# Attention pieces of four heads: the value product turned round onto two column tiles of the array

## The chip, the cores and the metric

The kernel runs on one core of a Trainium2 chip. The metric is the device time of one execution in microseconds (us). A core has a matrix engine (PE, with its weight loads listed apart as PEld), a vector engine (DVE), a scalar engine (ACT), a general engine (POOL, also called GpSimd) and a queue that issues transfers (SP). They run side by side and wait for each other through semaphores. On PE a product takes a stationary operand, loaded first, and a moving operand, streamed through it; the result lands in PSUM, from which DVE and ACT read. All other tiles lie in SBUF.

## The reference

Eight heads of causal attention over 8 batches of 576 positions (head dimension 64), four heads with a local window of 32, four with a strided mask, and then a two-layer network on the result.

```python
scores = scale * np.matmul(q, k.transpose(0, 1, 3, 2))
mask_local = (rel >= 0) & (rel < stride)
mask_strided = (rel >= 0) & (pos[None, :] % stride == pos[:, None] % stride)
...
scores = scores - np.max(scores, axis=-1, keepdims=True)
attn = np.exp(scores)
attn = attn / (np.sum(attn, axis=-1, keepdims=True) + 1e-09)
return np.matmul(attn, v).astype(np.float32)
...
h = x @ w_in                    # 4608 x 512 by 512 x 2048
sp = np.maximum(h, 0.0) + np.log1p(np.exp(-np.abs(h)))
g = h * erf(sp)
return (g @ w_out).astype(np.float32)
```

## The kernel before, in words

The network is cut into 12 chunks of 384 tokens, and each chunk into 16 slices of 128 hidden units: 192 steps, made by `ftile`. A step's `mm1` is 12 matrix products into a PSUM tile `h`. Eleven operations on ACT and DVE then work on the tiles `a` and `b` (DVE's are `n2`, `n5`, `n6`, `prod` and `split_lo`), and the result is split into a high part `ghi` (ACT) and a low part `glo` (DVE). A step's `mm2` is three times three products with `ghi` and `glo` stationary, into the three PSUM tiles `o`. There are three buffers of `h`: a fourth `mm1` can start only when `prod` (the last to read `h`, L682) has released the first.

Attention makes the network's input, `xhi` and `xlo`. Its masks leave only blocks near a diagonal (the strided heads after a reordering of positions), so a piece holds the scores of a few blocks of 96, 126 or 72 queries against 128 keys. Batches 0 and 1 go through `piece`, which is not altered beyond the names and sizes of buffers. Batches 2 to 7 go through `quad`: 36 pieces of four heads (two pairs), 18 with 96 queries to a block and 12 with 126 (two blocks to a pair, so eight head blocks, scores in two PSUM banks), and 6 with 72 queries (one block to a pair, four head blocks, one bank). Scores are stored with the keys on the partitions and the queries along the row, and a piece goes like this:

- `scores` (PE): in the two-bank pieces eight products, the two heads of a pair on the two 64-row tiles of the array.
- `mask` (DVE) adds the mask, `maxi` (POOL, a reduction over all partitions) takes the maximum over the keys, `sub` (DVE) subtracts it, `exp` (ACT).
- `av` (PE): the exponentials `sm` are stationary, the values `v` move. `v` has a 65th column of ones, so each product's last column is the sum of the exponentials. Queries come out on the partitions.
- `total`, `invert`, `scale` (DVE, for each pair): the sum plus 1e-9, its reciprocal, and the product of the two into `xn`.
- `transp` (PE): turns `xn` round, head dimensions onto the partitions, as `mm1` needs them.
- `split_hi` (ACT) and `split_lo_x` (DVE) write `xhi` and `xlo` from PSUM.

The order of all work is set by a planner in the kernel (`Plan`): every operation has a cost, a key and the operations it comes after, buffers are handed out by tag, and the planner lists each engine's instructions in the order of the starts that it works out. On the chip each engine then runs its list strictly in that order. Operations named in `TWO` (two SBUF operands on DVE) and POOL's are kept apart in the planned order (`locks`).

Of the kernel before, what the change touches and what calls it, by code (L numbers as in the profile page):

```python
# [18 lines left out]
P = 128  # L19
# [44 lines left out]
class Buf:  # L64
# [6 lines left out]
    def __getitem__(self, key):  # L71
        return self.tile[key]

# [95 lines left out]
def attention_moe(  # L169
# [31 lines left out]
    bufs = {"qk": 2, "v": 3, "sm": 3, "mx": 2, "xn": 2, "ps": 2, "h": 3, "a": 2, "b": 2, "ghi": 3, "glo": 3,  # L201
# [15 lines left out]
    def dve(n, x=1.0):  # L217
        return 0.067 + n * x / 960.0

    def act(n, fixed=0.093):  # L220
        return fixed + n / 1200.0


    def piece(b, hp, j, key, dt, ring, pe_mask=False, pool_sub=False, early=False):
# [168 lines left out]
    def quad(b, loc, j, key, dt, ring):  # L393
# [14 lines left out]
        sm = [buf("apool", "sm", [P, 4 * QS], f"sm{i}_{pid}") for i in range(nbank)]  # L408
        mx = [buf("apool", "mx", [P, 4 * QS], f"mx{i}_{pid}") for i in range(nbank)]
        pav = [buf("ps_a", "ps", [P, 512], f"av{i}_{pid}") for i in range(2)]  # L410
        xn = [buf("apool", "xn", [P, 4, D], f"xn{i}_{pid}") for i in range(2)]
        rc = [buf("apool", "r", [P, 4, 1], f"r{i}_{pid}") for i in range(2)]
        pt = buf("ps_a", "ps", [P, 512], f"t_{pid}")
# [79 lines left out]

        def av():
            for i in range(2):
                for u in range(units):
                    bank, c = place(i, u // 2, u % 2)
                    yield nc.tensor.matmul(  # L498
                        pav[i][:n, u * (D + 1) : (u + 1) * (D + 1)],
                        sm[bank][:, c : c + n],  # L500
                        v[i][:, u // 2, u % 2, :],
                        start=True,
                        stop=True,
                    )

        def norm(i):
            a, rr = lambda: pav[i][:n, : units * (D + 1)].rearrange("p (u d) -> p u d", u=units), lambda: rc[i][:n, :units]

            def total():
                yield nc.vector.tensor_scalar(  # L510
                    out=rr(), in0=a()[:, :, D : D + 1], scalar1=1e-9, scalar2=None, op0=ALU.add
                )

            def invert():
                yield nc.vector.reciprocal(rr(), rr())

            def scale():
                yield nc.vector.tensor_tensor(
                    out=xn[i][:n, :units], in0=a()[:, :, :D], in1=rr().broadcast_to([n, units, D]), op=ALU.mult
                )  # L520

            return total, invert, scale

        def transp():
            for i in range(2):
                for blk in range(nblk):
                    c = i * w + blk * n
                    yield nc.tensor.transpose(  # L528
                        pt[:, c : c + n], xn[i][:n, 2 * blk : 2 * blk + 2, :].rearrange("p h d -> p (h d)"), ident[:n, :n]
                    )  # L530

        def views(i, t):
            base, src = (b % 2) * S, pt[:, i * w : (i + 1) * w]
# [30 lines left out]
        o_v = add("pe", 0.00174 * n * 2 * units + 0.05, key + dt + 0.2, av, [*o_e, *lv], [*pav, *xn], [*sm, *v])  # L564
        o_n = []
        for i in range(2):
            total, invert, scale = norm(i)
            o = add("dve", 0.07, key + 1.5 * dt, total, [o_v], [rc[i]], [pav[i]])
            o = add("dve", 0.1, key + 1.5 * dt, invert, [o], [], [rc[i]])
            o_n.append(add("dve", dve(units * D), key + 1.5 * dt + 0.1, scale, [o], [], [pav[i], rc[i], xn[i]]))  # L570
        o_t = add("pe", 0.09 + 0.11 * 2 * nblk, key + 2 * dt, transp, o_n + ring, [pt], [*xn])
        done = []
        for i in range(2):
            hi, lo = split(i)
            o = add("act", act(w, 0.06), key + 2 * dt + 0.1, hi, [o_t], [], [pt])
            done.append(add("dve", dve(w), key + 2 * dt + 0.2, lo, [o], [], [pt]))
# [359 lines left out]
```

## Time and profile before

| | |
|---|---|
| median of 3 runs | 984.49 us (984.04 to 984.52) |
| profiled execution | 983.67 us, of which the span of its instructions is 981.9 us |
| PE busy | 970.0 us, 99% of the span |
| DVE busy | 720.9 us, 73% |
| ACT busy | 654.0 us, 67% |
| POOL busy | 146.4 us, 15% |
| granted PE clock | 1.00 throughout |

A row of the profile names line, engine, operation, output and inputs, shape, count, busy time and mean duration, and behind the last bar how long its engine stood idle before it and what ended that. Since records of one engine overlap (the next starts before the last one's end is written), a duration is a little longer than the time that an instruction adds; the distance from start to start in the timeline is what it adds. A product of plain 32-bit floats (`scores`, `av`) is recorded as two matmuls, a product of the network (on split parts) or a transpose as one.

### The profile page before, as it was taken

Reading aid. Unit: us, or ns where it says so; the run is one execution under the profiler, and the core shown is the slowest. Engines: PE = TensorE matmul, PEld = TensorE weight load, DVE = VectorE, ACT = ScalarE, POOL = GpSimd, SP = SyncE. Lnnn points to the kernel's source line nnn. Section 1 sums busy time; section 2 is a strip of 40 time slices with the busy share of each in tenths; the row PEclk is TensorE's granted clock in tenths of the full one; section 3 lists DMA queues with packets and bytes.
Section 4 is the critical chain, followed back from the end, with each engine's and each line's share of the span. In section 5 each row is a group of like instructions: output and inputs, shape, how many; then the busy total and the mean of one; then the engine's idle time right before and its main releaser. Section 6 shows DMA issues by size and latency. Waiting matters only on the chain.

```text
span 981.9 us, 15767 instructions
## 1 busy us (share of the span) xinstructions
PE 970.0 (99%) x5683; PEld 871.8 (89%) x5683; DVE 720.9 (73%) x1607; ACT 654.0 (67%) x1475; POOL 146.4 (15%) x94
## 2 busy tenths in 40 slices
PE   8999999999999999999999999999999999999998
PEld 6688989998899999899998989999999899999997
DVE  6999997776767777577778686667767776666664
ACT  4676777666757666666767666766756666766765
POOL 3534111111111311021011210111111210000000
PEclk9999999999999999999999999999999999999999
DMA  9994211012112221020221220211121210000000
GB/s 323 287 346 154 76 42 46 26 52 64 59 37 87 72 56 49 28 68 20 77 62 50 89 71 12 76 34 44 53 69 48 79 45 1 33 1 1 33 1 33
DMA packets 37661, 68.80 MB, mean 70 GB/s; under 512 B 4176, under 2 KB 18640, under 8 KB 37584
## 3 DMA queue, kind: packets, MB, share of 16 engines
q1 hardware_dynamic: 37584, 67.80, 21.6%
q8 instruction: 45, 0.74, 0.3%
q14 instruction: 32, 0.26, 0.1%
HBM read 58.34 MB, written 9.44 MB: 69 GB/s over the span
## 4 chain that ended last, share of the span: by engine, by line
PE 92%; DVE 6%; DMA 1%; issue 0%; ACT 0%; SPq 0%
PE h L647 40%; PE o L717 40%; PE av L498 5%; PE s L452 4%; DVE w L605 1%; DVE w L611 1%; PE t L528 1%; DVE pair L619 1%; DVE w L598 1%; PE s L265 1%; DMA words<-w_in 1%; PE av L308 1%; DVE xlo L362 0%; DVE a L652 0%; DMA qk<-qk_loc 0%; DVE b L652 0%
## 5 line engine op out<-in xcount | busy, mean ns | idle before, releaser
L717 PE MATMUL o<-pair,ghi 128*128 128x512 f32 x1152 | 364.2, 397 | 0.0
L647 PE MATMUL h<-xhi,pair 128*128 128x384 f32 x1536 | 305.5, 340 | 0.6 <-DVE b L682 0.6
L647 PEld LDWEIGHTS h<-xhi,pair 128*128 128x128 f32 x1536 | 271.2, 188 | 14.4 <-DVE b L682 1.6
L655 ACT ACTIVATE b<-b 128x384 f32<-128x384 f32 x384 | 198.9, 520 | 70.0 <-DVE b L652 67.8
L717 PEld LDWEIGHTS o<-pair,ghi 128*128 128x128 f32 x1152 | 208.5, 188 | 32.6
L717 PE MATMUL o<-pair,glo 128*128 128x512 f32 x576 | 225.2, 391 | 0.0
L476 POOL PARTITION_ALL_REDUCE mx<-sm x66 | 101.2, 1572 | 599.4 <-DVE sm L468 599.4
L647 PE MATMUL h<-xlo,pair 128*128 128x384 f32 x768 | 166.1, 337 | 0.0
L688 DVE TENSOR_TENSOR glo<-b,ghi 128x384 fp32r<-128x384 f32 x192 | 110.5, 576 | 60.7 <-ACT ghi L685 51.2
L685 ACT CAST ghi<-b 128x384 fp32r<-128x384 f32 x192 | 98.1, 511 | 79.3 <-PE o L717 73.1
L652 DVE SCALAR_TENSOR_TENSOR a<-h,a 128x384 f32<-128x384 f32 x192 | 106.2, 553 | 56.3 <-ACT a L655 55.4
L682 DVE TENSOR_TENSOR b<-b,h 128x384 f32<-128x384 f32 x192 | 105.1, 548 | 44.3 <-ACT b L655 43.9
L647 PEld LDWEIGHTS h<-xlo,pair 128*128 128x128 f32 x768 | 137.4, 187 | 0.0
L652 DVE SCALAR_TENSOR_TENSOR a<-a,h 128x384 f32<-128x384 f32 x192 | 105.5, 550 | 42.1 <-ACT b L655 40.3
L717 PEld LDWEIGHTS o<-pair,glo 128*128 128x128 f32 x576 | 108.1, 188 | 23.3
L655 ACT ACTIVATE b<-a 128x384 f32<-128x384 f32 x192 | 100.2, 522 | 40.2 <-DVE glo L688 39.2
L655 ACT ACTIVATE a<-h 128x384 f32<-128x384 f32 x192 | 92.9, 484 | 46.2 <-PE h L647 44.4
L655 ACT ACTIVATE a<-a 128x384 f32<-128x384 f32 x192 | 100.3, 522 | 35.1 <-DVE a L652 33.7
L652 DVE SCALAR_TENSOR_TENSOR b<-b,a 128x384 f32<-128x384 f32 x192 | 108.8, 567 | 3.1
L498 PEld LDWEIGHTS av<-v,sm 128*96 128x96 f32 (+2 forms) x528 | 54.2, 172 | 2.2
L291 POOL PARTITION_ALL_REDUCE mx<-sm x24 | 45.1, 1890 | 64.2 <-ACT sm L283 58.6
L498 PE MATMUL av<-v,sm 128*96 128x65 f32 (+2 forms) x528 | 53.3, 253 | 0.0
(48 smaller groups left out, 651.2 us busy)
## 6 DMA issues: line engine op xcount, KB each, us to landing
qk<-qk_loc SPq DMA_DIRECT2D x48, 304.0 KB, 3.1
qk<-qk_str SPq DMA_DIRECT2D x32, 380.0 KB, 3.7
v<-v_all SPq DMA_DIRECT2D x80, 130.0 KB, 2.2
out<-ob SPq DMA_DIRECT2D x36, 256.0 KB, 2.0
words<-w_in SPq DMA_DIRECT2D x16, 512.0 KB, 5.9
words<-w_out SPq DMA_DIRECT2D x16, 512.0 KB, 6.1
qk<-qk_str SPq DMA_DIRECT2D x16, 136.0 KB, 2.1
v<-v_all SPq DMA_DIRECT2D x16, 65.0 KB, 1.9
```

The costliest lines, as they stand in the source:

```text
L265: yield nc.tensor.matmul(dst, qk[:, k0 + blk * step : k0 + blk * step + P], qk[:, blk * 2 * n : (blk + 1) * 2 * n], start=blk == 0, stop=n ...
L291: yield nc.gpsimd.partition_all_reduce(mx[:, :cols], sm[:, :cols], P, ReduceOp.max)
L452: yield nc.tensor.matmul(s[bank][:, c : c + width], qk[i][rows, keys], qk[i][rows, q0 : q0 + width], start=bank not in used, stop=True, sk ...
L476: yield nc.gpsimd.partition_all_reduce(mx[k][:, :cols], sm[k][:, :cols], P, ReduceOp.max)
L498: yield nc.tensor.matmul(pav[i][:n, u * (D + 1) : (u + 1) * (D + 1)], sm[bank][:, c : c + n], v[i][:, u // 2, u % 2, :], start=True, stop= ...
L647: yield nc.tensor.matmul(ph[:, :CH], win[4 * s + cc][:, w, fs], x[cc][:, c0 : c0 + CH], start=(i == 0), stop=(i == len(terms) - 1))
L652: yield nc.vector.scalar_tensor_tensor(out=out, in0=in0, scalar=scalar, in1=in1, op0=op0, op1=op1)
L655: yield nc.scalar.activation(dst, src, func, bias=bias[i], scale=scale)
L682: yield nc.vector.tensor_tensor(out=bb.tile, in0=bb.tile, in1=ph[:, :CH], op=ALU.mult)
L685: yield nc.scalar.copy(ghi.tile, bb.tile)
L688: yield nc.vector.tensor_tensor(out=glo.tile, in0=bb.tile, in1=ghi.tile.bitcast(F32), op=ALU.subtract)
L717: yield nc.tensor.matmul(po.tile, g[:, ts], wout[f][:, w], start=(f == 0 and i == 0), stop=(f == NFC - 1 and i == 2),)
```

## The change: what it does

In `quad` the value product is turned round. `v` (128 keys by 64 columns, without the ones) is stationary and the exponentials move; the two heads of a pair write to partitions 0 to 63 and 64 to 127 of one PSUM tile `px`, so they use the two 64-column tiles of the array in turn. The result has head dimensions on the partitions already, and `transp` goes. The sums come from POOL: a second reduction over all partitions, `add` in place of `max`, on the exponentials of each bank, into `su`. Every partition then holds the same row of sums. DVE turns the sums by 32x32 transposes (`gather`, 64 partitions at a time), adds 1e-9 and takes the reciprocal of one column per block (`invert`), and spreads the result over the rows with one more transpose (`spread`). One DVE product (`scale`) writes the normalised piece from PSUM into the SBUF tile `tt`, and `split_hi` and `split_lo_x` read `tt` instead of PSUM. That an earlier chunk has been read out of `xhi` and `xlo` (`ring`) is now waited for by `split_hi` on ACT, where it was by `transp` on PE. `ghi` and `glo` go from three buffers to two; `tt` and `inv` share two.

```diff
-    bufs = {... "xn": 2, "ps": 2, "h": 3, "a": 2, "b": 2, "ghi": 3, "glo": 3,
+    bufs = {... "tt": 2, "ps": 2, "h": 3, "a": 2, "b": 2, "ghi": 2, "glo": 2,
...
+        def total(k):
+                yield nc.gpsimd.partition_all_reduce(su[k][:, :cols], sm[k][:, :cols], P, ReduceOp.add)
+        def gather(h):
+                if pos > n:
+                    yield nc.vector.memset(t[rows, cols : cols + pos - n], 1.0)
...
+                for u in range(2 * nblk):
+                    yield nc.vector.transpose(
+                        tt[rows, u * pos : (u + 1) * pos], t[rows, lo + u * step : lo + u * step + pos]
+                    )
+        def invert():
+            yield nc.vector.tensor_scalar(
+                out=rc[:, :nb, 0], in0=tt[:, :width].rearrange("p (c k) -> p c k", k=32)[:, :, 0],
+                scalar1=1e-9, scalar2=None, op0=ALU.add,
+            )
+            yield nc.vector.reciprocal(rc[:, :nb], rc[:, :nb])
+        def spread():
+            yield nc.vector.transpose(
+                inv[:, :width].rearrange("p (c k) -> p c k", k=32), rc[:, :nb].broadcast_to([P, nb, 32])
+            )
         def av():
             for i in range(2):
-                    yield nc.tensor.matmul(
-                        pav[i][:n, u * (D + 1) : (u + 1) * (D + 1)],
-                        sm[bank][:, c : c + n], v[i][:, u // 2, u % 2, :], start=True, stop=True)
+                for blk in range(nblk):
+                    for h in range(2):
+                        bank, c = place(i, blk, h)
+                        c0 = (i * nblk + blk) * n
+                        yield nc.tensor.matmul(
+                            px[h * D : (h + 1) * D, c0 : c0 + n], v[i][:, blk, h, :D], sm[bank][:, c : c + n],
+                            start=True, stop=True)
-        def norm(i):          # total, invert, scale for each pair
-        def transp():         # nc.tensor.transpose(pt[...], xn[i][...], ident)
+        def scale():
+            yield nc.vector.tensor_tensor(
+                out=tt[:, : 2 * w]..., in0=px[:, : 2 * w]..., in1=inv[:, :width]...[:, :, :n], op=ALU.mult)
...
-            o = add("act", act(w, 0.06), key + 2 * dt + 0.1, hi, [o_t], [], [pt])
+            o = add("act", act(w), key + 2 * dt + 0.1, hi, [o_x] + ring, [], [tt])
```

`pos` is `n` rounded up to a multiple of 32 (96, 128, 96) and `width` is `2 * nblk * pos` (384, 512, 192). Per piece there are eight transposes in `gather` (four in the pieces of 72), and two fills of the columns beyond `n` where `n` is not a multiple of 32.

On PE, the value product of the piece of batch 4, local heads, second column (`4_0_1`) before; each row of L498 stands there twice in turn, `av` is its PSUM tile, `t` the tile of the transposes, `o` those of `mm2`:

```order
L717 MATMUL o_3_3696<-pair_1865,glo_4361 128x512
L498 MATMUL av_4_0_1_4493<-v_4_0_1_4141,sm_4_0_1_4376 96x65
L498 MATMUL av_4_0_1_4493<-v_4_0_1_4141,sm_4_0_1_4377 96x65
L498 MATMUL av_4_0_1_4494<-v_4_0_1_4247,sm_4_0_1_4376 96x65
L498 MATMUL av_4_0_1_4494<-v_4_0_1_4247,sm_4_0_1_4377 96x65
L717 MATMUL o_3_3648<-pair_1932,ghi_4387 128x512 x2
L717 MATMUL o_4_4596<-pair_694,glo_4475 128x512
L528 MATMUL t_0_1_4601<-ident,xn_4_0_1_4495 128x96 x2
L528 MATMUL t_0_1_4601<-ident,xn_4_0_1_4496 128x96 x2
L717 MATMUL o_4_4562<-pair_734,ghi_4507 128x512 x2
```

And after, the same piece on PE (`x` is `px`; each row of L551 again stands twice in turn):

```order
L755 MATMUL o_3_3748<-pair_1939,glo_4480 128x512
L551 MATMUL x_0_1_4539<-sm_4_0_1_4413,v_4_0_1_4211 64x96
L551 MATMUL x_0_1_4539<-sm_4_0_1_4414,v_4_0_1_4211 64x96
L551 MATMUL x_0_1_4539<-sm_4_0_1_4413,v_4_0_1_4287 64x96
L551 MATMUL x_0_1_4539<-sm_4_0_1_4414,v_4_0_1_4287 64x96
L755 MATMUL o_4_4554<-pair_694,ghi_4518 128x512 x2
```

One group of PE work for a piece's values is left of two, and it writes 64 rows by 96 columns eight times instead of 96 by 65.

On DVE, the normalisation of the same piece before, between the operations of the network's steps:

```order
L688 TENSOR_TENSOR glo_4511<-b_4412,ghi_4507 128x384
L510 TENSOR_SCALAR r_4_0_1_4518<-av_4_0_1_4493 96x4
L510 TENSOR_SCALAR r_4_0_1_4520<-av_4_0_1_4494 96x4
L515 RECIPROCAL r_4_0_1_4518<-r_4_0_1_4518 96x4
L515 RECIPROCAL r_4_0_1_4520<-r_4_0_1_4520 96x4
L518 TENSOR_TENSOR xn_4_0_1_4495<-av_4_0_1_4493,r_4_0_1_4518 96x256
L652 SCALAR_TENSOR_TENSOR a_4446<-a_4446,h_4420 128x384
L518 TENSOR_TENSOR xn_4_0_1_4496<-av_4_0_1_4494,r_4_0_1_4520 96x256
L652 SCALAR_TENSOR_TENSOR b_4522<-b_4522,a_4446 128x384
```

After, on DVE, the same piece:

```order
L525 STREAM_TRANSPOSE tt_0_1_4509<-su_4_0_1_4500 64x96 x4
L726 TENSOR_TENSOR glo_4529<-b_4444,ghi_4518 128x384
L525 STREAM_TRANSPOSE tt_0_1_4509<-su_4_0_1_4507 64x96 x4
L720 TENSOR_TENSOR b_4497<-b_4497,h_4382 128x384
L533 TENSOR_SCALAR r_0_1_4558<-tt_0_1_4509 128x12
L537 RECIPROCAL r_0_1_4558<-r_0_1_4558 128x12
L690 SCALAR_TENSOR_TENSOR a_4466<-a_4466,h_4428 128x384
L726 TENSOR_TENSOR glo_4582<-b_4497,ghi_4562 128x384
L690 SCALAR_TENSOR_TENSOR b_4552<-b_4552,a_4466 128x384
L690 SCALAR_TENSOR_TENSOR a_4567<-h_4483,a_4567 128x384
L541 STREAM_TRANSPOSE inv_0_1_4510<-r_0_1_4558 128x384
L557 TENSOR_TENSOR tt_0_1_4509<-x_0_1_4539,inv_0_1_4510 128x384
```

Six instructions for the two pairs have become twelve, spread over more of the network's operations, with four transposes in a row between two of them.

More of the change, by code (lines that the diff above doesn't have):

```diff
@@ L72, in __getitem__, with __init__ @@
         return self.tile[key]
+class View:
+    def __init__(self, buf, how, part, **sizes):
+        self.buf, self.how, self.part, self.sizes = buf, how, part, sizes
+    def __getitem__(self, key):
+        return self.buf[:, self.part].rearrange(self.how, **self.sizes)[key]
 TWO = {"n6", "sub", "split_lo"}
@@ L199, in attention_moe @@
     bias = (B1, B3, B4, B7, Q0)
-    bufs = {"qk": 2, "v": 3, "sm": 3, "mx": 2, "xn": 2, "ps": 2, "h": 3, "a": 2, "b": 2, "ghi": 3, "glo": 3,
+    bufs = {"qk": 2, "v": 3, "sm": 3, "mx": 2, "tt": 2, "ps": 2, "h": 3, "a": 2, "b": 2, "ghi": 2, "glo": 2,
             "ob": 3, "r": 2}
@@ L407, in quad @@
         s = [buf("ps_a", "ps", [P, 512], f"s{i}_{pid}") for i in range(nbank)]
[L408 to L413, printed above, removed]
+        sm = [buf("apool", "sm", [P, 512], f"sm{i}_{pid}") for i in range(nbank)]
+        mx = [buf("apool", "mx", [P, 512], f"mx{i}_{pid}") for i in range(nbank)]
+        su = [buf("apool", "mx", [P, 512], f"su{i}_{pid}") for i in range(nbank)]
+        pos = 32 * (-(-n // 32))
+        width = 2 * nblk * pos
+        tt = buf("apool", "tt", [P, 512], f"tt_{pid}")
+        inv = buf("apool", "tt", [P, 512], f"inv_{pid}")
+        rc = buf("apool", "r", [P, 16, 1], f"r_{pid}")
+        px = buf("ps_a", "ps", [P, 512], f"x_{pid}")
         def place(i, blk, h):
@@ L492, in exp, with run @@
             return named("exp", run)
+        def total(k):
+            def run():
+                yield nc.gpsimd.partition_all_reduce(su[k][:, :cols], sm[k][:, :cols], P, ReduceOp.add)
+            return named("total", run)
+        def gather(h):
+            def run():
+                rows, t = slice(h * D, (h + 1) * D), su[h % nbank]
+                if pos > n:
+                    yield nc.vector.memset(t[rows, cols : cols + pos - n], 1.0)
+                if nbank == 2:
+                    lo, step = 0, n
+                else:
+                    lo, step = h * n, 2 * n
+                for u in range(2 * nblk):
+                    yield nc.vector.transpose(
+                        tt[rows, u * pos : (u + 1) * pos], t[rows, lo + u * step : lo + u * step + pos]
+                    )
+            return named("gather", run)
@@ L494, in av @@
         def av():
             for i in range(2):
-                for u in range(units):
-                    bank, c = place(i, u // 2, u % 2)
-                    yield nc.tensor.matmul(
-                        pav[i][:n, u * (D + 1) : (u + 1) * (D + 1)],
[L500 to L504, printed above, removed]
-        def norm(i):
[L507 to L522, printed above, removed]
@@ L524, in transp @@
-        def transp():
-            for i in range(2):
-                for blk in range(nblk):
[L527 to L530, printed above, removed]
+                for blk in range(nblk):
+                    for h in range(2):
[3 more added lines that the diff above has]
+                            px[h * D : (h + 1) * D, c0 : c0 + n], v[i][:, blk, h, :D], sm[bank][:, c : c + n],
+                            start=True, stop=True,
+                        )
@@ L563, in quad @@
             o_e.append(add("act", act(cols), key + dt + 0.1 + 0.01 * k, exp(k), [o], [], [sm[k]]))
[L564 to L571, printed above, removed]
+        o_g = []
+        for k in range(nbank):
+            o = add("pool", 0.4 + cols * 0.0028, key + dt + 0.15 + 0.01 * k, total(k), [o_e[k]], [su[k]], [sm[k]])
+            o_g.append(o)
+        n_g = 2 * nblk * (0.067 + pos / 960.0) + (0.06 if pos > n else 0.0)
+        o = None
+        for h in range(2):
+            k = h % nbank
+            o = add("dve", n_g, key + 1.3 * dt + 0.01 * h, gather(h), [o_g[k]] + ([o] if o else []), [tt, inv] if h == 0 else [], [su[k], tt])
+        o = add("dve", 0.27, key + 1.3 * dt + 0.05, invert, [o], [rc], [tt])
+        o_i = add("dve", dve(width), key + 1.3 * dt + 0.06, spread, [o], [], [rc, inv])
+        d_v = (1.2 if n > QL else 0.98) if nblk == 2 else 0.6
+        o_v = add("pe", d_v, key + 1.5 * dt, av, [*o_e, *lv], [px], [*sm, *v])
+        o_x = add("dve", dve(2 * w), key + 1.5 * dt + 0.1, scale, [o_v, o_i], [], [px, inv, tt])
         done = []
```

28 lines of the change are left out of this document (18 added, 10 removed).

## The prediction

> **What bounds the kernel now.** I read the page's first part, then the groups of instructions with their shapes kept apart, the timeline of PE, the stretches of time, and the waits.
>
> ```profile
> PE 970.0 (99%) x5683; PEld 871.8 (89%) x5683; DVE 720.9 (73%) x1607; ACT 654.0 (67%) x1475; POOL 146.4 (15%) x94
> L682 DVE TENSOR_TENSOR b<-b,h 128x384 f32<-128x384 f32 x192 | 105.1, 548 | 44.3 <-ACT b L655 43.9
> 120.00:812.00 692.00, 692.00 (x4115) 626.86 (x4114) 506.57 (x1141) 459.81 (x1019) 101.19 (x66) 1.00 0.18 55
> PE h L647 <- DVE b L682: 0.6, 1, 0.6
> PEld h L647 <- DVE b L682: 1.6, 4, 0.9
> ```
>
> The third row is the stretch in which all four-head pieces run (busy PE, PEld, DVE, ACT, POOL): PE has no idle time in 692 us, DVE is busy 506.57, 73%. PE's waits for DVE's release of an `h` buffer come to 2.2 us in the whole run. So PE's work is the time, and what is taken from PE is gained as long as the others keep ahead of it.
>
> **PE, before.** The timeline of PE shows each kind of small group between products of 128x512; the counts are in the groups.
>
> ```profile
> 340.94 0.62 PE L717 MATMUL o<-pair,ghi 128*128 128x512 f32 x2
> ...
> 341.63 1.49 PE L498 MATMUL av<-v,sm 128*96 128x65 f32 x16
> 342.94 0.71 PE L717 MATMUL o<-pair,ghi 128*128 128x512 f32 x2
> ...
> 343.71 0.62 PE L717 MATMUL o<-pair,ghi 128*128 128x512 f32 x2
> ...
> 344.39 0.62 PE L717 MATMUL o<-pair,ghi 128*128 128x512 f32 x2
> ...
> 345.08 0.49 PE L528 MATMUL t<-ident,xn 96*128 96x96 f32 x4
> 345.36 0.70 PE L717 MATMUL o<-pair,ghi 128*128 128x512 f32 x2
> ...
> 346.13 0.62 PE L717 MATMUL o<-pair,ghi 128*128 128x512 f32 x2
> 346.83 0.62 PE L717 MATMUL o<-pair,ghi 128*128 128x512 f32 x2
> ...
> 347.62 1.14 PE L452 MATMUL s<-qk 64*128 64x96 f32 x16
> 348.68 0.73 PE L717 MATMUL o<-pair,ghi 128*128 128x512 f32 x2
> ...
> 349.48 0.69 PE L647 MATMUL h<-xhi,pair 128*128 128x384 f32 x3
> ```
>
> ```profile
> 305.02 0.59 PE L528 MATMUL t<-ident,xn 126*128 126x126 f32 x4
> 305.37 0.71 PE L717 MATMUL o<-pair,ghi 128*128 128x512 f32 x2
> ...
> 425.78 1.87 PE L498 MATMUL av<-v,sm 128*126 128x65 f32 x16
> 427.46 1.64 PE L647 MATMUL h<-xhi,pair 128*128 128x384 f32 x8
> ...
> L498 PE MATMUL av<-v,sm 128*96 128x65 f32 x288 | 26.9, 246 | 0.0
> L498 PEld LDWEIGHTS av<-v,sm 128*96 128x96 f32 x288 | 27.2, 165 | 1.1
> L498 PE MATMUL av<-v,sm 128*126 128x65 f32 x192 | 22.4, 270 | 0.0
> L498 PE MATMUL av<-v,sm 128*72 128x65 f32 x48 | 4.0, 227 | 0.0
> ```
>
> Three products of 512 take 0.68 us (343.71 to 344.39). The 96-wide value group takes 1.31 (341.63 to 342.94), and the triple behind it 0.77 in place of 0.68: 1.40 in all. Its transposes take 0.28 and the triple behind them 0.09 more: 0.37. For 126 the same reading gives 1.68 + 0.09 and 0.35 + 0.09, 2.21 together. The 16 records of a value group go at 0.082 and 0.105 us each, which is 0.00084 us for each stationary column (96, 126); for 72, eight records of 0.060 and 0.09 make 0.57, with two transposes 0.76 (estimates from that pace). Counts divided by records make 18, 12 and 6 pieces: 18 x 1.77 + 12 x 2.21 + 6 x 0.76 = 62.9 us.
>
> **PE, after.** No row shows 64-column tiles. The nearest is the score group, which runs on two 64-row tiles: 347.62 to 348.68, 0.10 more than usual ahead of it (346.83 to 347.62) and 0.12 behind, 1.28 in all. With 128 stationary columns at 0.00084 a load takes 0.107; eight pairs of records, loads of a pair side by side, are 0.85, and 0.43 is left for entering and leaving the tiled mode. I take this overlap and this 0.43 for the column tiles too. A pair there loads 64 columns (0.054) and moves 96, 126 or 72 (0.081, 0.106, 0.060 at the same price a column), so moving sets the pace: 8 x 0.081 + 0.43 = 1.08, 8 x 0.106 + 0.43 = 1.28, and 4 x 0.060 + 0.43 = 0.67. That is 18 x 1.08 + 12 x 1.28 + 6 x 0.67 = 38.8, so **PE saves 24.1 us**. Ends: changeover as in the untiled groups (0.09) saves 36; each group as dear as the score group (1.28, and half the pairs, 0.86, for 72) saves 19; no overlap of the two tiles at all (16 records in a row plus 0.43) saves 1.
>
> **DVE.** It loses and gains work that no PE time shows, as long as it stays ahead.
>
> ```profile
> L510 DVE TENSOR_SCALAR r<-av 96x4 f32<-96x4 f32 x36 | 4.3, 150 | 1.4 <-PE av L498 1.4
> L515 DVE RECIPROCAL r<-r 96x4 f32<-96x4 f32 x36 | 4.5, 162 | 0.0
> L518 DVE TENSOR_TENSOR xn<-av,r 96x256 f32<-96x256 f32 x36 | 14.0, 414 | 0.0
> L549 DVE TENSOR_TENSOR xlo<-t,xhi 128x192 fp32r<-128x192 f32 x36 | 11.3, 352 | 14.8 <-ACT xhi L544 14.6
> L549 DVE TENSOR_TENSOR xlo<-t,xhi 128x72 fp32r<-128x72 f32 x12 | 2.4, 226 | 0.2 <-ACT xhi L544 0.2
> L468 DVE TENSOR_TENSOR sm<-s,con 128x384 f32<-128x384 f32 x36 | 18.7, 552 | 0.7 <-PE s L452 0.7
> ...
> 425.94 0.55 DVE L652 SCALAR_TENSOR_TENSOR a<-a,h 128x384 f32<-128x384 f32 x1
> 426.40 0.55 DVE L652 SCALAR_TENSOR_TENSOR a<-h,a 128x384 f32<-128x384 f32 x1
> ```
>
> Removed: 2 x (0.150 + 0.162 + 0.414) = 1.45 us a piece, 0.9 in the short ones. A transpose is unpriced; by the two L549 rows an operation costs about 0.15 and 0.00105 a column, so 0.25 for 96 columns and 0.285 for 128. Its ends are 0.15 (a four-column L510) and 0.552 (a full 384-column row). Added to a 96 piece: 8 x 0.25, 0.31 to invert, 0.55 to spread, 0.55 to scale, 3.41; to a 126 piece 8 x 0.285, two fills 0.30, 0.31 and 2 x 0.68, 4.25; to a 72 piece about 2.3. Net 18 x 1.96 + 12 x 2.80 + 6 x 1.4 = 77 us, all in the stretch from 120 to 812.
>
> **POOL** gets 66 more reductions; `add` is priced as `max`. Its own share goes from 15% to about 27%, no bound. But it holds DVE up:
>
> ```profile
> 265.57 2.83 POOL L476 PARTITION_ALL_REDUCE mx<-sm  x2 [19.26 <-DVE sm L468]
> 267.03 1.19 DVE L483 TENSOR_TENSOR sm<-sm,mx 128x384 f32<-128x384 f32 x1 [0.22 <-POOL mx L476]
> L476 POOL PARTITION_ALL_REDUCE mx<-sm x66 | 101.2, 1572 | 599.4 <-DVE sm L468 599.4
> L483 DVE TENSOR_TENSOR sm<-sm,mx 128x384 f32<-128x384 f32 x36 | 23.9, 673 | 3.3 <-POOL mx L476 3.2
> L688 DVE TENSOR_TENSOR glo<-b,ghi 128x384 fp32r<-128x384 f32 x192 | 110.5, 576 | 60.7 <-ACT ghi L685 51.2 <-PE t L528 8.8
> L652 DVE SCALAR_TENSOR_TENSOR b<-b,a 128x384 f32<-128x384 f32 x192 | 108.8, 567 | 3.1
> ```
>
> A subtraction from two SBUF tiles that meets a reduction takes 1.19 us; L682, with one operand in PSUM, averages 0.548, L688 and L652 on two SBUF tiles 0.576 and 0.567, L483 0.673. Over 0.548 that is 5.4 + 3.6 + 4.5 us, 13.5 for 66 reductions, 0.2 each; 66 more cost DVE another 14 (`split_lo_x` now reads two SBUF tiles too and isn't in `TWO`). The Trainium skill (SBUF — State Buffer, Terms) says that the port pair which the two engines share is locked for the whole instruction and the loser fully blocked. Here the trace differs: the second reduction ends at 268.40 (265.57 + 2.83), the subtraction, 0.55 long when alone, already at 268.22, so it was let in before the reduction ended; by the page it would have ended at 268.95, 1.4 us late in place of 0.64, and the 14 us would be about 30.
>
> DVE in the stretch: 506.6 + 77 + 14 = 598 us in 692 - 24 = 668, 89% by records, but two L652 rows start 0.46 apart and last 0.55, so about 75 to 80% by starts. It stays ahead on average, with less slack. PE's waits for it (2.2 us) should grow with twice the collisions and with the free share falling from 27% to 11%: a factor of 2 to 5, 4 to 11 us, of which 2.2 is there. I add 4; ends 0 and 20.
>
> **The rest.** Two buffers of `ghi` and `glo` make ACT's split wait for the `mm2` two steps back; covered as long as `mm2` runs soon after its `glo`, and inside the 4. `split_hi` on ACT waits for `ring`: the step's tanh and square stand behind it, so an uncovered wait would reach PE through `prod`; the cover is that the chunk in question is read out before the piece is turned. Reading SBUF instead of PSUM adds under 0.05 us to each of 72 ACT splits. PSUM loses three tiles a piece and gains one; transfers are the same. Sum: 983.67 - 24.1 + 4 = 963.6; the median stands 0.8 above the profiled run, so **964 us**.
>
> **Rivals.**
> *Loads that don't hide.* If a weight load on one column tile cannot run under a product on the other, a pair costs two loads and one move, 0.108 + 0.081 = 0.189 (0.214, 0.168): groups of 1.94, 2.14 and 1.10, 67.6 us in all, 4.7 more than now, and with the waits 984.5 + 4.7 + 4 = 993. It decides from a pair of 0.167 in the 96 pieces (1.77 = 8 pairs + 0.43). Against it: the 96-wide rows move on at 0.082 us while their loads have 0.165 written for each, so loads do run under products, in the same rows of the array. The Trainium skill (TensorE: Matmul & The Clock Gate, Part 3, packing small matmuls) says a load overlaps running products only where the row group differs, which two column tiles never do; the L498 rows, all on 128 rows, don't bear it out.
> *The tiles take turns.* Loads hide but products don't overlap: saves 1 us, 984.5 - 1 + 4 = 987.
> *DVE sets the pace.* 264 transposes (30 pieces of 8, 6 of 4): at 0.25 more each, they add 66 us and DVE's records fill 664 of 668 us; waits of 20 us, 980. At 0.4 more, 704 against 692: 1000. For it: in-order DVE with four transposes in a row ahead of `glo` and `prod`. Against it: shapes of 64x96 are small.
> *Cheap tiles.* Untiled changeovers and no waits: 984.5 - 36 = 949.
>
> **Chances.** Forecast (955 to 972) 0.70; loads that don't hide 0.05; tiles take turns 0.04; DVE sets the pace 0.14, half of it still below 982; cheap tiles 0.07. The range 953 to 980 leaves out the first two rivals, half of the third and most of the fourth. A change of 0.2% is about what can be told from none. Faster 0.85, same 0.03, slower 0.12.
>
> **What would show it.** Right: 16-record groups of 64x96 of about 1.1 us from start to start with their changeovers, no transposes on PE, PE at 98% or more, DVE transposes of 0.25 us, two-SBUF rows of DVE 0.02 to 0.1 us longer. Wrong: groups of 1.7 and more, or idle time of PE ended by DVE `b` (the release of `h`) or by `glo`, above 10 us, with transposes of 0.4 us or reductions longer than 1.57.

## The result, and the profile after

The changed kernel takes 994.48 us (median of 4 runs, 993.32 to 995.27) against 984.50 for the kernel before on the same chip: ratio 1.0098, 95% interval 1.0081 to 1.0116. The forecast was 964 with a range to 980, so it is wrong by 30 us and in the sign. The profiled execution took 995.27 us, its span 993.5.

First the page of the changed kernel: busy time of each engine, the chain that ended last by engine, and the groups that matter.

```profile
PE 958.1 (96%) x5551; PEld 830.8 (84%) x5551; DVE 833.0 (84%) x1835; ACT 655.5 (66%) x1475; POOL 332.7 (33%) x160
...
PE 53%; DVE 33%; ACT 7%; POOL 3%; issue 3%; DMA 0%; SPq 0%; DVEq 0%; POOLq 0%; ACTq 0%
...
L490 POOL PARTITION_ALL_REDUCE mx<-sm x66 | 102.4, 1591 | 353.4 <-DVE sm L482 349.1
L510 POOL PARTITION_ALL_REDUCE su<-sm x66 | 183.1, 2805 | 85.8 <-ACT sm L504 85.8
...
L726 DVE TENSOR_TENSOR glo<-b,ghi 128x384 fp32r<-128x384 f32 x192 | 123.5, 643 | 35.2 <-ACT ghi L723 34.9
L690 DVE SCALAR_TENSOR_TENSOR b<-b,a 128x384 f32<-128x384 f32 x192 | 136.5, 712 | 2.5
...
L720 DVE TENSOR_TENSOR b<-b,h 128x384 f32<-128x384 f32 x192 | 104.1, 542 | 26.3 <-ACT b L693 25.8
```

The chain by engine in the kernel before, for comparison:

```profile
PE 92%; DVE 6%; DMA 1%; issue 0%; ACT 0%; SPq 0%
```

PE's busy time fell by 12 us, but its idle time grew from 11.9 (981.9 - 970.0) to 35.4 us, and the chain now runs through DVE for a third of the span, where it was 6%. The busy time is not work alone: for the same list of products it is 944.6 us in the kernel with `max` below, so 13.5 of the 958.1 us are records that took longer. The two reductions of the same tiles differ: the maxima (L490) average 1.59 us, the sums (L510) 2.81. L690 and L726, which read two SBUF tiles, went from 0.567 and 0.576 us to 0.712 and 0.643; L720, with one operand in PSUM, did not change.

The stretch from 120 to 812 us (busy PE, PEld, DVE, ACT, POOL), and then two rows of the waits (us in total, times, longest):

```profile
120.00:812.00 692.00, 669.13 (x3919) 577.86 (x3918) 604.40 (x1330) 454.98 (x1004) 272.16 (x126) 1.00 0.17 54
```

```profile
PEld h L685 <- DVE b L720: 40.0, 59, 2.9
...
PE h L685 <- DVE b L720: 19.7, 29, 2.7
```

PE, which had no idle time there, has 23 us of it. PE waits 19.7 us for `prod` to release an `h` buffer, where it was 0.6, and the weight loads 40.0 us (partly the same time), where it was 1.6.

Part of the rise is the clock, which was granted at 1.00 throughout before. Here PE's two longest waits, 2.74 us up to 139.81 and 2.55 us up to 809.75, are each followed by some us at about half of it. First PE's timeline there, then two stretches of time, where the granted clock is the third figure from the end:

```profile
139.81 2.70 PE L685 MATMUL h<-xhi,pair 128*128 128x384 f32 x8 [2.73 <-DVE b L720]
142.31 1.42 PE L685 MATMUL h<-xlo,pair 128*128 128x384 f32 x4
...
809.75 1.94 PE L551 MATMUL x<-sm,v 128*64 128x126 f32 x14 [2.55 <-ACT sm L504]
811.62 2.93 PE L685 MATMUL h<-xhi,pair 128*128 128x384 f32 x8
```

```profile
140.00:144.00 4.00, 4.00 (x14) 3.94 (x14) 3.90 (x13) 1.68 (x4) 0.00 (x0) 0.57 0.01 4
810.00:816.00 6.00, 6.00 (x28) 5.67 (x27) 4.65 (x17) 2.48 (x7) 2.97 (x1) 0.51 0.15 36
```

Eight products into `h`, 1.51 us from start to start at 147.49, take 2.50 and 2.72 there. Over both stretches that adds about 4.3 us (an estimate from such distances), beside a net loss of 10. Both waits stand behind an `add`. Ahead of the second, two `n6` under an `add` take 2.98 us and push back `sub`, `exp` and so the value product. Ahead of the first, an operation that unpacks weights (L636, with one operand in SBUF) takes 1.89 us under an `add`, where its median is 0.41, and stands with four transposes before `prod`. So the hold is not confined to operations on two SBUF tiles.

### The profile page after: what moved, and what is told of

It reads as the page before. It is cut to its first block, busy times and chain, and to the rows that moved or that the text cites. A ratio compares the mean times of both kernels' runs of the same rounds, so it can differ in the third digit from the quotient of the medians.

```text
span 993.5 us, 15748 instructions
## 1 busy us (share of the span) xinstructions
PE 958.1 (96%) x5551; PEld 830.8 (84%) x5551; DVE 833.0 (84%) x1835; ACT 655.5 (66%) x1475; POOL 332.7 (33%) x160
## 4 chain that ended last, share of the span: by engine, by line
PE 53%; DVE 33%; ACT 7%; POOL 3%; issue 3%; DMA 0%; SPq 0%; DVEq 0%; POOLq 0%; ACTq 0%
PE h L685 27%; PE o L755 22%; DVE a L690 6%; DVE b L690 5%; DVE glo L726 4%; DVE b L720 3%; POOL su L510 3%; ACT b L693 3%; DVE tt L525 2%; PE s L466 2%; DVE w L649 2%; DVE w L643 2%; DVE pair L657 1%; DVE sm L497 1%; ACT a L693 1%
## 5 line engine op out<-in xcount | busy, mean ns | idle before, releaser
L685 PE MATMUL h<-xhi,pair 128*128 128x384 f32 x1536 | 310.9, 345 | 21.4 <-DVE b L720 19.7
L685 PEld LDWEIGHTS h<-xhi,pair 128*128 128x128 f32 x1536 | 267.9, 189 | 52.3 <-DVE b L720 40.0
L490 POOL PARTITION_ALL_REDUCE mx<-sm x66 | 102.4, 1591 | 353.4 <-DVE sm L482 349.1
L510 POOL PARTITION_ALL_REDUCE su<-sm x66 | 183.1, 2805 | 85.8 <-ACT sm L504 85.8
L726 DVE TENSOR_TENSOR glo<-b,ghi 128x384 fp32r<-128x384 f32 x192 | 123.5, 643 | 35.2 <-ACT ghi L723 34.9
L690 DVE SCALAR_TENSOR_TENSOR b<-b,a 128x384 f32<-128x384 f32 x192 | 136.5, 712 | 2.5
L690 DVE SCALAR_TENSOR_TENSOR a<-h,a 128x384 f32<-128x384 f32 x192 | 105.1, 547 | 33.8 <-ACT a L693 32.8
L690 DVE SCALAR_TENSOR_TENSOR a<-a,h 128x384 f32<-128x384 f32 x192 | 104.3, 544 | 27.5 <-ACT b L693 25.5
L720 DVE TENSOR_TENSOR b<-b,h 128x384 f32<-128x384 f32 x192 | 104.1, 542 | 26.3 <-ACT b L693 25.8
L302 POOL PARTITION_ALL_REDUCE mx<-sm x24 | 47.3, 1985 | 64.2 <-ACT sm L294 58.6
L525 DVE STREAM_TRANSPOSE tt<-su 64x96 f32<-64x96 f32 (+1 forms) x264 | 53.5, 255 | 9.7 <-POOL su L510 8.3
```

The costliest lines, as they stand in the source:

```text
L302: yield nc.gpsimd.partition_all_reduce(mx[:, :cols], sm[:, :cols], P, ReduceOp.max)
L490: yield nc.gpsimd.partition_all_reduce(mx[k][:, :cols], sm[k][:, :cols], P, ReduceOp.max)
L510: yield nc.gpsimd.partition_all_reduce(su[k][:, :cols], sm[k][:, :cols], P, ReduceOp.add)
L525: yield nc.vector.transpose(tt[rows, u * pos : (u + 1) * pos], t[rows, lo + u * step : lo + u * step + pos])
L685: yield nc.tensor.matmul(ph[:, :CH], win[4 * s + cc][:, w, fs], x[cc][:, c0 : c0 + CH], start=(i == 0), stop=(i == len(terms) - 1))
L690: yield nc.vector.scalar_tensor_tensor(out=out, in0=in0, scalar=scalar, in1=in1, op0=op0, op1=op1)
```

## The experiments

Three theories were put up. **A**: the second reduction is the loss; an `add` over the partitions takes longer than a `max` and holds up DVE's operations on two SBUF tiles (`n6`, `split_lo`, `sub`), and behind them `prod`, the release of `h` and PE. **B**: DVE's added work for the normalisation is too much, or the splits that read SBUF are. **C**: the order is the loss; the planner priced `total` as it prices a `max`, so its lists don't fit the chip.

### max in place of add

```diff
-                yield nc.gpsimd.partition_all_reduce(su[k][:, :cols], sm[k][:, :cols], P, ReduceOp.add)
+                yield nc.gpsimd.partition_all_reduce(su[k][:, :cols], sm[k][:, :cols], P, ReduceOp.max)
```

> The changed kernel with the second reduction taken as max in place of add (so the sums of the normalisation are left out); everything else is the same, the planned order too. Theory A (the add reduction itself: it lasts 2.81 us on average against 1.59 for max, and holds back DVE's operations on two SBUF tiles): the reductions shrink by 66 x 1.2 = 80 us of POOL, the rows glo and b<-b,a of DVE fall from 0.643 and 0.712 to about 0.59, PE's 60 us of waits for b fall to 20 or less, and the time to 958 to 972 us. Theory B (DVE's own added work of 264 transposes and the rest sets the pace): DVE keeps that work, 985 to 995 us.

Measured: 963.42 us, ratio to before 0.9771 (0.9754 to 0.9788). Every list of instructions is that of the changed kernel, one operation of POOL apart, and the time is 31 us shorter. A held, also in its side forecasts: L726 and L690 fall to 0.594 and 0.602 us, the waits of PE and its loads for `b` from 59.7 to 17.2. B fell as the cause of the loss: all its work is still there. PE's longest wait is 1.37 us here and the clock doesn't fall before the end, so some 4 of the 31 us are the clock. The same place in both kernels shows how; first the changed kernel's timeline, picked from POOL, DVE, ACT and PE in turn:

```profile
326.72 3.19 POOL L510 PARTITION_ALL_REDUCE su<-sm  x1 [1.79 <-ACT sm L504]
...
326.81 2.99 DVE L690 SCALAR_TENSOR_TENSOR b<-b,a 128x384 f32<-128x384 f32 x2
...
329.37 0.52 ACT L693 ACTIVATE b<-b 128x384 f32<-128x384 f32 x1 [2.74 <-DVE b L690]
...
330.79 0.54 DVE L720 TENSOR_TENSOR b<-b,h 128x384 f32<-128x384 f32 x1
...
331.38 1.32 PE L685 MATMUL h<-xhi,pair 128*128 128x384 f32 x6 [0.76 <-DVE b L720]
```

and the kernel with `max`:

```profile
319.03 1.76 POOL L510 PARTITION_ALL_REDUCE su<-sm  x1 [1.97 <-ACT sm L504]
...
319.12 1.81 DVE L690 SCALAR_TENSOR_TENSOR b<-b,a 128x384 f32<-128x384 f32 x2
...
321.92 0.54 DVE L720 TENSOR_TENSOR b<-b,h 128x384 f32<-128x384 f32 x1
...
322.77 1.55 PE L685 MATMUL h<-xhi,pair 128*128 128x384 f32 x8
```

Two `n6` start 0.09 us after the reduction. Under the `add` they take 2.99 us together, under the `max` 1.81; `prod` (L720) follows 4.0 and 2.8 us behind the first of them. In the first kernel PE then stands 0.76 us; in the second the next `mm1` starts with no wait recorded ahead of it. Single records give the hold. In the changed kernel an `n6` that starts 0.09 us into an `add` of 3.19 us takes 2.52, and one 0.32 us into one of 2.51 takes 1.76; alone it takes 0.55. So DVE is let in about 2.07 us after the start of the long `add` (two other records give 2.07) and 1.53 after that of the shorter. The same reading with `max` gives 0.88 us of 1.76 and 0.69 of 1.42.

### The true price of the sums in the planner

```diff
-            o = add("pool", 0.4 + cols * 0.0028, key + dt + 0.15 + 0.01 * k, total(k), ...)
+            o = add("pool", 0.34 + cols * 0.00567, key + dt + 0.15 + 0.01 * k, total(k), ...)
```

> The changed kernel with one number of the planner corrected: the price of the second reduction, 0.34 + 0.00567 a column (2.51 us at 384 and 3.19 at 504, as measured) in place of 0.4 + 0.0028. The instructions are the same, their order is not. Theory A without a share of the order: the reductions last as long and collide as often, 988 to 997 us. Theory C (the lists were drawn up for reductions that end a microsecond earlier, so DVE's strict order puts operations on two SBUF tiles into them and piles work behind them): 965 to 982 us, PE's waits for b halved. Theory B: 985 to 995 us.

Measured: 977.15 us, ratio 0.9918 (0.9903 to 0.9933). `n6` in the page and PE's wait for `prod`:

```profile
L690 DVE SCALAR_TENSOR_TENSOR b<-b,a 128x384 f32<-128x384 f32 x192 | 135.9, 709 | 2.7
...
PE h L685 <- DVE b L720: 10.7, 15, 1.5
```

The same instructions in another order are 17 us faster, so C has a large share. L690 stays at 0.709 and L726 at 0.642, so DVE is held as long as before; PE's wait for `prod` falls from 19.7 to 10.7 us. The better order doesn't avoid the holds, it makes fewer of them end in a wait of PE. PE's longest wait is 1.66 us and the clock doesn't fall before the end, so about 4 of the 17 us are again the clock.

### The splits read PSUM again

```diff
-                out=tt[:, : 2 * w].rearrange("p (u q) -> p u q", q=n),
+                out=px[:, : 2 * w].rearrange("p (u q) -> p u q", q=n),
...
-            base, src = (b % 2) * S, tt[:, i * w : (i + 1) * w]
+            base, src = (b % 2) * S, px[:, i * w : (i + 1) * w]
```

> The changed kernel with scale writing back into the PSUM tile px in place of the SBUF tile tt, and the two splits reading px. Theory D (a share of the loss is the splits: the 24 strided ones on ACT went from 0.376 to 0.665 us and on DVE from 0.416 to 0.749, and the DVE ones now read two SBUF tiles): the ACT split returns to about 0.38 and the DVE split to about 0.42, 7 and 8 us less work, time 984 to 991 us. Theory A alone: within 3 us of the changed kernel, 991 to 997 us.

Measured: 983.61 us, ratio 0.9983 (0.9971 to 0.9994), 10.9 us under the changed kernel and just below the range of the expectation's theory D, which gave the splits a share. Groups by shape, of the changed kernel and then of this one:

```profile
L581 DVE TENSOR_TENSOR xlo<-tt,xhi 128x252 fp32r<-128x252 f32 x24 | 17.4, 749 | 0.8 <-ACT xhi L576 0.8
...
L576 ACT CAST xhi<-tt 128x252 fp32r<-128x252 f32 x24 | 15.2, 665 | 1.8 <-DVE tt L557 0.8 <-PE h L685 0.8
...
L576 ACT CAST xhi<-tt 128x192 fp32r<-128x192 f32 x36 | 11.4, 347 | 2.6 <-DVE tt L557 2.3
```

```profile
L576 ACT CAST xhi<-x 128x192 fp32r<-128x192 f32 x36 | 10.3, 321 | 11.5 <-DVE x L557 11.1
...
L581 DVE TENSOR_TENSOR xlo<-x,xhi 128x252 fp32r<-128x252 f32 x24 | 9.2, 414 | 0.0
...
L576 ACT CAST xhi<-x 128x252 fp32r<-128x252 f32 x24 | 8.1, 377 | 3.9 <-DVE x L557 3.3
```

The splits of the strided heads (252 columns, read at a stride of 18 elements) take 0.29 us more on ACT and 0.34 more on DVE from SBUF than from PSUM (on DVE some of it is holds, since `xlo` now comes from two SBUF tiles); those read in a row (192) take 0.03 more. The run doesn't separate that work from the order, which also changes, since the planner has another price for the splits and other lifetimes of `tt` and `px`. Nor does it separate it from the clock, which falls once here instead of twice (at 139 us, behind a wait of 2.74).

### Add reductions in the kernel before

A second reduction is put after each exponential in the kernel before; nothing reads it.

```diff
+        su = [buf("apool", "mx", [P, 4 * QS], f"su{i}_{pid}") for i in range(nbank)]
...
+                yield nc.gpsimd.partition_all_reduce(su[k][:, :cols], sm[k][:, :cols], P, ReduceOp.add)
...
+            add("pool", 0.4 + cols * 0.0028, key + dt + 0.15 + 0.01 * k, extra(k), [o_e[k]], [su[k]], [sm[k]])
```

> The kernel before with nothing but the 66 add reductions of the exponentials added on POOL, at the changed kernel's prices in the planner; nobody reads their result. Theory A: DVE's glo and b<-b,a rows lengthen, PE, 100% busy before, begins to wait for b, and the time rises by 8 to 20 us, 992 to 1005 us. Theory B: PE and DVE have the same work as before, so the time stays within 3 us of 984.5.

Measured: 1010.81 us, ratio 1.0253 (1.0236 to 1.0270): right for A in kind, but above the 1005 us that A gave at most. Two rows of its page and two of its waits:

```profile
L497 POOL PARTITION_ALL_REDUCE su<-sm x66 | 185.9, 2835 | 106.1 <-ACT sm L491 102.5 <-DVE glo L697 3.1
L661 DVE SCALAR_TENSOR_TENSOR b<-b,a 128x384 f32<-128x384 f32 x192 | 131.6, 686 | 3.0
```

```profile
PEld h L656 <- DVE b L691: 23.7, 28, 1.9
PE h L656 <- DVE b L691: 15.6, 17, 1.5
```

Nothing of the turned product or of the new normalisation is in this kernel, and the same pattern is: `n6` long, PE waiting for `prod`. The 66 reductions cost 25.6 us where DVE had 27% of its time free.

### Max reductions in the kernel before, and the true price there

The kernel of the last section with `max`:

```diff
-                yield nc.gpsimd.partition_all_reduce(su[k][:, :cols], sm[k][:, :cols], P, ReduceOp.add)
+                yield nc.gpsimd.partition_all_reduce(su[k][:, :cols], sm[k][:, :cols], P, ReduceOp.max)
```

> The kernel before with 66 reductions of the exponentials added on POOL as with the add reductions (1010.8 us), but by max; nobody reads their result. Theory A (it is the add reduction's length and hold, not that there are twice as many): 984 to 990 us. Rival (twice the number of reductions is enough): 995 us or more.

Measured: 987.87 us, ratio 1.0038 (1.0023 to 1.0053). The number of reductions is worth 3.6 us, their length the other 22.

With `add` and the true price:

```diff
-            add("pool", 0.4 + cols * 0.0028, key + dt + 0.15 + 0.01 * k, extra(k), ...)
+            add("pool", 0.34 + cols * 0.00567, key + dt + 0.15 + 0.01 * k, extra(k), ...)
```

> The kernel before with the 66 unread add reductions, priced in the planner as they were measured (0.34 + 0.00567 a column). Theory C (most of the loss comes from an order drawn up for shorter reductions): 1010.8 falls to 988 to 998 us. If the hold on DVE counts whatever the order is: 1004 to 1012 us.

Measured: 997.80 us, ratio 1.0138 (1.0122 to 1.0153), at the upper edge of what C gave. Of the 25.6 us, 13 are the order and about as much remains with the price right.

### Both corrections, and two more constants of the planner

The true price and the splits from PSUM together, both edits as above:

```diff
+            o = add("pool", 0.34 + cols * 0.00567, key + dt + 0.15 + 0.01 * k, total(k), ...)
...
+            base, src = (b % 2) * S, px[:, i * w : (i + 1) * w]
```

> The changed kernel with both the planner's price of the second reduction corrected and the scaled piece kept in PSUM. If the two shares are separate (the order, 17 us, and the splits, 11 us), 994.5 - 17 - 11 = 964 to 969 us. If both act through the same thing (DVE's operations on two SBUF tiles meeting the reductions), less than the sum: 970 to 976 us.

Measured: 979.77 us, ratio 0.9947 (0.9930 to 0.9964), 2.6 us more than the price alone: both expectations missed, the two gains do not add. PE's two main waits are both longer than with the price alone: 12.0 us for `prod` (10.7), and 6.7 for `glo` (1.9).

The same with two more constants of the planner: the latency that it takes ahead of POOL's work, and `ADT`, which spaces the stages of a piece.

```diff
-ASH, ADT = -0.644, 1.759
+ASH, ADT = -0.644, 1.5
...
-    LATENCY = {"pe": 0.25, "act": 0.2, "dve": 0.15, "pool": 0.6, "sp": 0.1}
+    LATENCY = {"pe": 0.25, "act": 0.2, "dve": 0.15, "pool": 0.3, "sp": 0.1}
```

> As the kernel with both corrections, and the planner told two more things: that a reduction starts 0.3 us after DVE's write in place of 0.6 (the trace shows 0.17 from end to start), and the pieces' operations keyed by 1.5 steps in place of 1.759. The instructions are the same. Theory C (what is left of PE's waits is the order): 956 to 966 us. If the length of the reductions alone is what is left: within 3 us of the kernel with both corrections.

Measured: 972.25 us, ratio 0.9882 (0.9867 to 0.9897), faster than both kernels, short of what was expected. Then `ADT` at 1.3:

```diff
-ASH, ADT = -0.644, 1.5
+ASH, ADT = -0.644, 1.3
```

> The best version so far (true price of the add reductions, splits from PSUM, the planner's latency of POOL 0.3, distance ADT 1.5) with ADT 1.3. The work is the same, only the order differs. If an order is as good as its prices (theory C, strict form): within 3 us of it, 969 to 976. If orders with the same prices still scatter by which operation meets a hold: anywhere from 965 to 982, and the difference shows as PE's waits for b (14.8 us there), not as PE's busy time.

Measured: 968.67 us, ratio 0.9833 (0.9810 to 0.9856), the best version of all. It lies just below the range of the strict form of C and inside that of the other, so the time alone doesn't decide between them. PE's wait for `prod` rose here (from 3.3 to 5.4 us, on the loads from 11.5 to 12.0) and the one for `glo` stayed, so the expectation on where it would show missed. Three orders of the same work, 968.7, 972.3 and 979.8, differ by 11 us. The operations' costs in the planner are the same in all three; `ADT` differs, and the latency of POOL is 0.6 in the slowest and 0.3 in the others.

### The holds in an order made for them

The 972.25 us version with `max` in the second reduction, its order unchanged; the sums are left out again:

```diff
-                yield nc.gpsimd.partition_all_reduce(su[k][:, :cols], sm[k][:, :cols], P, ReduceOp.add)
+                yield nc.gpsimd.partition_all_reduce(su[k][:, :cols], sm[k][:, :cols], P, ReduceOp.max)
```

> The best version so far with max instead of add in the second reduction (so the normalisation does not divide by the sum) and an unchanged order: the order was made for reductions of the length of add, the holds are those of max. If what the add holds still cost in this order is small, since the order was made for them: 966 to 971 us against 972. If the holds cost wherever they lie: 956 to 965, PE's waits for b falling from 14.8 us to under 8 and b<-b,a from 0.74 to 0.60 us.

Measured: 963.03 us, ratio 0.9788 (0.9763 to 0.9814). The time is in the second range; PE's waits are not, at 3.3 and 9.1 us. L690 goes from 0.739 to 0.612. This makes a square:

| order | `add` | `max` | difference |
|---|---|---|---|
| of the changed kernel | 994.48 | 963.42 | 31.1 |
| of the 972 us version | 972.25 | 963.03 | 9.2 |

With short reductions the two orders are worth the same; with long ones they differ by 22 us. The other differences between the two (the splits from PSUM are in the second row alone) are, taken together, worth nothing that can be told when the reduction is short.

### No second reduction

The transposes read the maxima; the planner has 66 operations fewer.

```diff
-        su = [buf("apool", "mx", [P, 512], f"su{i}_{pid}") for i in range(nbank)]
+        su = mx
...
-            o = add("pool", 0.4 + cols * 0.0028, key + dt + 0.15 + 0.01 * k, total(k), [o_e[k]], [su[k]], [sm[k]])
-            o_g.append(o)
+            o_g.append(o_e[k])
```

> The changed kernel without the second reduction at all: the transposes read the row of maxima instead, so the normalisation of batches 2 to 7 divides by something that is not the sum, and the planner has 66 POOL operations fewer to place. Theory A (the 66 add reductions hold DVE's operations with two SBUF operands off, and that is the loss): 954 to 964 us, the time of the kernel with max reductions or some us less, PE's waits for b (release of h) under 15 us in all, b<-b,a at 0.57 to 0.60 us. Theory B (DVE's 77 us of added work, or the splits from SBUF, are a large part of the loss): 970 us or more, with PE waiting over 25 us for b or glo.

Measured: 957.74 us, ratio 0.9727 (0.9707 to 0.9748). The first line of its page, then `n6` and a strided split by shape, then two rows of the waits:

```profile
PE 943.1 (99%) x5551; PEld 828.3 (87%) x5551; DVE 781.5 (82%) x1835; ACT 657.5 (69%) x1475; POOL 149.1 (16%) x94
```

```profile
L689 DVE SCALAR_TENSOR_TENSOR b<-b,a 128x384 f32<-128x384 f32 x192 | 105.9, 552 | 2.4
...
L576 ACT CAST xhi<-tt 128x252 fp32r<-128x252 f32 x24 | 14.8, 667 | 0.1
```

```profile
PEld h L684 <- DVE b L719: 8.7, 22, 1.1
...
PE h L684 <- DVE b L719: 1.7, 3, 0.8
```

The transposes, the spread, the scaling and the slow splits from SBUF are all in it, DVE is busy 82%, and the kernel is 26.7 us faster than before: all that PE saves (26.3 us, below) comes out. B is excluded as a cause by itself. The edit also gives the maxima the buffers that they shared with the sums (tag `mx`); with `max` they are still shared, and that, the short reductions and the other order together are 963.42 - 957.74 = 5.7 us.

### Two buffers of ghi and glo

In the kernel before:

```diff
-    bufs = {... "ghi": 3, "glo": 3,
+    bufs = {... "ghi": 2, "glo": 2,
```

> The kernel before, with two buffers of ghi and glo instead of three, and nothing else. If the third buffers were worth nothing, as the prediction had it: 983 to 987 us (ratio within 0.002 of 1), and the waits of the split that writes ghi and of the one that writes glo for mm2 stay under 2 us in all. If a part of the loss of the changed kernel is the two buffers (ACT or DVE held up until an mm2 has read its tile): 988 us or more, with PE's added waits ended by ghi and glo.

Measured: 985.37 us, ratio 1.0011 (1.0000 to 1.0022). The bound on the waits of the splits was wrong (ACT waits 70.4 us for `mm2` ahead of `ghi`), but with three buffers it already waits 73.1 there, and it costs nothing. The third buffers are worth about 1 us, 2 at most.

## Why the prediction was wrong, step by step

- **PE's saving: right in kind, 8% small.** The predicted 24.1 us is 26.3 by the trace. The timeline of PE shows the groups on the column tiles for 126, 96 and 72 columns, with an untiled triple ahead of the second and one behind it:

```profile
333.69 1.08 PE L551 MATMUL x<-sm,v 128*64 128x126 f32 x16
334.70 1.68 PE L685 MATMUL h<-xhi,pair 128*128 128x384 f32 x8
...
348.67 0.61 PE L755 MATMUL o<-pair,ghi 128*128 128x512 f32 x2
349.12 0.39 PE L755 MATMUL o<-pair,glo 128*128 128x512 f32 x1
349.44 0.88 PE L551 MATMUL x<-sm,v 128*64 128x96 f32 x16
350.25 0.73 PE L755 MATMUL o<-pair,ghi 128*128 128x512 f32 x2
350.82 0.39 PE L755 MATMUL o<-pair,glo 128*128 128x512 f32 x1
351.05 0.63 PE L755 MATMUL o<-pair,ghi 128*128 128x512 f32 x2
...
362.36 0.47 PE L551 MATMUL x<-sm,v 128*64 128x72 f32 x8
362.76 0.73 PE L755 MATMUL o<-pair,ghi 128*128 128x512 f32 x2
```

  Sixteen records of 96 columns take 0.81 us (349.44 to 350.25), with 0.09 more than usual ahead (349.12 to 349.44 against 0.23) and 0.12 behind (350.25 to 351.05 against 0.68): 1.02, where 1.08 was forecast. With the same changeovers 126 takes 1.22 and 72 takes 0.61: 18 x 1.02 + 12 x 1.22 + 6 x 0.61 = 36.7 against the 62.9 of before. From 96 to 126 columns a group grows from 0.81 to 1.01, which is 0.00083 us a column for each pair of records, the pace that was forecast; 0.17 of the 0.81 is left over. So the changeover is 0.17 + 0.21, about 0.38 where 0.43 was taken from the score group, and that is the whole difference. The rivals "loads don't hide" and "the tiles take turns" are out: the first has 0.189 us for two records and the second about 0.16, and two records go every 0.10 with their loads, changeover included. That 994.5 lies next to the 993 of "loads don't hide" is chance. (The groups of that rival add up to 67.3 us, not 67.6.) The page "TensorE: Matmul & The Clock Gate" of the Trainium skill (Part 3, packing small matmuls), by which a load overlaps running products only where the row group differs, is not borne out by this pace.

- **DVE's own work: right in kind, a little large.** Transposes, spread, scaling and fills by shape:

```profile
L525 DVE STREAM_TRANSPOSE tt<-su 64x96 f32<-64x96 f32 x168 | 32.2, 243 | 6.0 <-POOL su L510 5.3
...
L525 DVE STREAM_TRANSPOSE tt<-su 64x128 f32<-64x128 f32 x96 | 21.3, 276 | 3.7 <-POOL su L510 3.0
...
L541 DVE STREAM_TRANSPOSE inv<-r 128x384 f32<-128x384 f32 x18 | 10.3, 572 | 0.3
L557 DVE TENSOR_TENSOR tt<-x,inv 128x384 f32<-128x384 f32 x18 | 9.9, 549 | 0.3
...
L519 DVE MEMSET su<- 64x2 f32 x24 | 1.4, 60 | 0.6
```

  0.243 and 0.276 us a transpose against 0.25 and 0.285; fills 0.06 against 0.15. In the kernel without the second reduction DVE is busy 60.6 us more than before (781.5 - 720.9), where 77 was forecast. Most of the gap is overlap, which busy time counts once: 168 transposes of 0.243 us are 40.8, of which 32.2 are busy time, and 96 of 0.276 are 26.5, of which 21.3 are. (A 72 piece adds up to 2.0 by the forecast's own prices, not 2.3.) The mechanism of the rival "DVE sets the pace" (long transposes) did not occur, though the time fell into its range.

- **"`add` is priced as `max`": the step that failed.** Of the prediction's signs that would show it wrong, two are seen: idle time of PE ended by the release of `h` (19.7 us), and longer reductions. The term had no row behind it and, unlike the other unseen costs, no bounds. The `add` takes 2.51 and 3.19 us where the `max` takes 1.42 and 1.76. The 14 us that DVE was to lose to collisions became, on `n6`, `split_lo` and the two larger shapes of `sub` alone (busy time after less before), 27.7 + 13.0 + 6.1 = 46.8.

- **"I add 4; ends 0 and 20" for PE's waits: failed with it.** DVE's busy time in the stretch came out at 604 us against 598 forecast, so the average share was right and told nothing: the sum has less own work and far more holds. A hold of 1.5 to 2.1 us falls on one operation of a chain, and PE stands when the three buffers of `h` don't cover it; how much they cover was not measured by itself. Add for `max` in this order is worth 31.1 us, where the whole term was to be 4; some 4 of it are the fallen clock behind the two longest waits, which the prediction doesn't have at all. The reductions themselves, at the length of `max`, cost 963.42 - 957.74 = 5.7 us, orders not being the same, which is near what the term was meant for.

- **The planner's order: not in the prediction at all.** The price in `total`'s `add` call is the changed kernel's own. In this kernel the true price alone gives back 17.3 us, and the two better orders, with the splits from PSUM, 22.2 and 25.8.

- **"Under 0.05 us" for reading SBUF: wrong for the strided heads** (0.29 us on ACT, 0.34 on DVE for the 24 splits of 252 columns, 0.10 and 0.07 for the 12 of 72), right for the 36 of the local heads. What it costs is not settled: 10.9 us came back with PSUM sources at the wrong price of the sums (in an order of its own, and with one fall of the clock less), 2.6 were lost with the price corrected, and 957.74 was reached with SBUF sources. The two buffers of `ghi` and `glo` cost nothing worth speaking of, as forecast.

- **The rule of the Trainium skill's page "SBUF — State Buffer" (Terms)**, a port pair locked for the whole instruction: the measured hold is 2.07 us of an `add` of 3.19 and 0.88 of a `max` of 1.76, so DVE was let in before the end again. By that rule the 14 us would have been about 30, as the prediction worked out, which is nearer to the 46.8 measured.

Open stays why three orders with the same costs of operations differ by 11 us, and why the true price takes waits away from PE while DVE's operations are held as long. Whether the rest between 968.67 and 957.74 can be won was not tried.

## What to carry to other kernels

A reduction over partitions on POOL is not one instruction with one price: measure the operation that will run before summing, and count what it holds up by the longest single hold against the slack of the chain behind it, not by an average share of busy time. Where a planner's prices set the order, a new operation at a wrong price costs twice, by itself and by the lists; correct the price first, then judge the idea. When a term of a sum has no row in the trace, the row of a like operation is one end of its range and not its value.

## What the runs showed of the hardware beyond that

- `partition_all_reduce` on 128 rows of plain floats: `add` 2.51 us at 384 columns and 3.19 at 504, `max` 1.42 and 1.76. A DVE operation on two SBUF tiles is let in after 1.53 and 2.07 us, and 0.69 and 0.88.
- A DVE operation with one operand in SBUF can be held too: L636 (128x512, uint32) took 1.89 us under an `add`, where its median is 0.41. The 264 transposes (L525) were not: none took over 0.31, though some ran under an `add` (three at 809.99).
- Two heads on two column tiles: a product of 96 columns (two records) adds 0.08 us, its load included, and entering and leaving cost a group about 0.38, of which 0.21 show ahead of it and behind it.
- In the changed kernel and the one with splits from PSUM, PE's three waits above 2.5 us (2.74, 2.55, 2.74) were each followed by a granted clock of 0.50, for 3 to 6 us; three waits of 2.23 us in the kernel with both corrections were not. In the 972 us version two shorter waits close together (1.64 and 1.18 us, at 60 and 63 us) were followed by it too, so the runs give no threshold.
- Reading SBUF at a stride of 18 elements on ACT takes 0.665 us for 252 columns, against 0.377 from PSUM at the same stride.
